# Linear attention with two expert layers: the sums over keys with features stationary, and a new plan

## The chip, the core and the metric

One core of a Trainium2 chip runs the whole program in one launch. TensorE (PE) multiplies matrices, VectorE (DVE), ScalarE (ACT) and GpSimd (POOL) do elementwise work, SyncE (SP) issues most loads and stores. The metric is device time in microseconds, the median of several runs.

## The reference

```python
def phi(x):
    proj = np.einsum('bhsd,df->bhsf', x, w_phi)
    proj = proj - np.max(np.abs(proj), axis=-1, keepdims=True)
    return np.concatenate([np.exp(proj), np.exp(-proj)], axis=-1)
q_p, k_p = (phi(q), phi(k))
kv = np.einsum('bhsf,bhsd->bhfd', k_p, v)
z = np.sum(k_p, axis=2)
num = np.einsum('bhsf,bhfd->bhsd', q_p, kv)
den = np.einsum('bhsf,bhf->bhs', q_p, z)[..., None] + 1e-06
x = num / den
...
h = x @ w_in
x = (h - np.tanh(h)) @ w_out
...
for e in range(E):
    h = np.maximum(x @ w1[e], 0.0)
    out += p[:, e:e + 1] * (h @ w2[e])
```

There are 4 batches, 8 heads, 576 positions and a head dimension of 64; `w_phi` has 128 columns, so a key or query has 256 features (128 of exp(+) and 128 of exp(-)). The attention output, 2304 tokens by 512, goes through a layer of 2048 hidden units and then through four experts of 1024, weighted by normalised probabilities. Everything is float32. `kv` and `z` are what this document calls the sums over keys: per head, 256 features by 64 value columns and one column of plain feature sums.

## The kernel before

The program has two parts. The first, attention and the layer with tanh, is not written in the order in which it runs. The code calls `add` (on the class `Issue`) for every step: its engine, an estimated duration, a function that emits its instructions, the steps it depends on, the ring buffers and PSUM banks it holds, and a mode of TensorE's array ("rows" for matmuls on half of the array's rows, "columns" for half of its columns, "all" otherwise). `Issue.run` then plays the graph through with those estimates and emits the instructions in the order in which the steps start there. Where several steps of one engine are ready, the one with the lowest key goes first; the keys come from the table `DUE`, one number for each step in the order of the `add` calls. A change of array mode is given `SWITCH` us there, and where TensorE is idle in that play between 5 and 45 us, `fill` emits dummy matmuls of the identity, one for each `T_FILL` (0.22 us). The second part, the experts, is written out by hand after `g.run()`.

`k_task(b, p)` handles the keys of two heads (a pair) of one batch: 16 tasks. It loads k and v, transposes k, projects it with `wphi` (a head on each half of the rows), takes the largest absolute value per key, subtracts it and takes both exponentials into `kp` (four keys a partition, 512 keys) and `kpr` (the other 64 keys of both heads). Then come the sums. In `mmk` the values are the stationary operand, 64 columns wide, one head on each half of the array's columns, and the features move, 256 wide: five matmuls a head. For `z`, VectorE first adds the features of four keys into `ks` (three additions a head, through the helper `tt`) and `mmz` multiplies the result with `ones`; in three tasks of the first batch (`SUM_0 = (0,)` leaves out p = 1, 2, 3) `mmz_all` multiplies all features with `ones` instead. The result lies with value columns on the partitions; ScalarE copies it to `kvT`, four transposes (`back`) bring features onto the partitions, and two copies write `kv`, whose last two columns are `z`.

`q_task(b, s, p)` handles the queries of a pair over half of the positions (320 or 256): 32 tasks. `mm(ab, x)` forms numerators and denominators: stationary are up to 64 queries' features on a half of the columns, moving are the 66 columns of `kv`. It is one step for exp(+) (`ea`) and one for exp(-) (`eb`). `moe_slot` and `moe_x2` are the first layer's steps, `split3` its three matmuls for each product (line 454 in the profile, whatever calls it). Line 335 is the helper that issues loads and stores, line 326 the helper for additions on VectorE.

Of the kernel before, what the change touches and what calls it, by code (L numbers as in the profile page):

```python
# [9 lines left out]
F32 = mybir.dt.float32  # L10
# [32 lines left out]
K_SUM = ['DVE', 'DVE', 'DVE']  # L43
K_BIAS = ((), (), (), ())
R_BIAS = (0, 0, 0, 0)
SUM_0 = (0,)
# [63 lines left out]

class Buf:
    def __init__(self, t, last, users):
        self.t, self.last, self.users = t, last, users


class Issue:

    HOP = {"PE": 0.055, "ACT": 0.037, "DVE": 0.033, "POOL": 0.08, "SP": 0.1}  # L120
    DRAIN = {"PE": 0.16, "ACT": 0.11, "DVE": 0.082, "POOL": 0.035, "SP": 0.0}
    SWITCH = 0.125
    T_FILL = 0.22
    fill = None

    def __init__(self, banks, lent):

        self.nodes, self.free_banks, self.lent = [], list(range(banks)), banks
        self.free_lent, self.n_lent = list(range(banks, banks + lent)), lent

    def add(self, eng, dur, fn, deps=(), due=0.0, bufs=(), bank=None, banks=(), frees=(), busy=None, early=0.0, home=False, mode="all", port=False, wire=False):
        x = Node()
        x.home, x.mode, x.port, x.wire = home, mode, port or eng == "POOL", wire or eng == "SP"
        x.eng, x.dur, x.busy, x.fn, x.banks, x.key = eng, dur, busy or dur, fn, [bank] if bank else list(banks), (due, len(self.nodes))
# [131 lines left out]
def attention_moe_moe_kernel(  # L266
# [65 lines left out]
    def dma(pairs, deps=(), due=0.0, bufs=(), early=0.0, slow=1.0, queue="SP"):  # L332
# [5 lines left out]
        return add(queue, size / 300e3, fn, deps, due, bufs, busy=0.7 * len(pairs), early=early, wire=True)  # L338


    ident = const.tile([128, 128], F32, name="ident")
    wphi = const.tile([128, 128], F32, name="wphi")
    b_m = const.tile([128, 1], F32, name="b_m")
    ones = const.tile([128, 3, 64], F32, name="ones")

    warm = const.tile([128, 24], F32, name="pad")[:, 0:1]
    edge.tile([128, 24], F32, name="pad_right")
    vtiles = [att.tile([128, 10 * 64], F32, name=f"vbuf{i}") for i in range(2)]

    make_identity(nc, ident)  # L350
    for _ in range(WARM):
        PE.matmul(accs[0][:, 0:128], lhsT=ident, rhs=ident, start=True, stop=True)
    DVE.memset(b_m, THETA2)
    DVE.memset(ones, 1.0)
    DVE.memset(ones[64:128, 1], 0.0)
    DVE.memset(ones[0:64, 2], 0.0)
    for vb in vtiles:
# [909 lines left out]
```

## Time and profile before

| | |
|---|---|
| median of 3 runs | 1376.47 us (1376.26 to 1376.79) |
| the profiled execution | 1376.24 us |
| its span, first to last instruction | 1374.5 us |
| TensorE busy | 1362.8 us, 99% |
| VectorE, ScalarE, GpSimd busy | 69%, 49%, 47% |
| granted TensorE clock, mean | 0.999 |

The span is what the instructions cover, the rest of the execution's time lies around it. Busy time counts an engine as busy while at least one of its instructions runs. Matmuls are pipelined and overlap in the records, so what a group of them costs is read from its first start to the start of what follows, not from the length of the records. A matmul of float32 operands leaves two records, a transpose one.

### The profile page before, as it was taken

How to read it: one execution, taken by the hardware profiler on the slowest of the kernel's cores; microseconds unless marked ns; L12 is line 12 of the kernel's file. 1: busy time of each engine (PE TensorE's matmuls, PEld its weight loads, DVE VectorE, ACT ScalarE, POOL GpSimd, SP SyncE). 2: the span in 40 equal slices, each digit the busy share in tenths (PEclk: the TensorE clock that was granted, in tenths of full speed). 3: DMA queues.
4: the chain of work that ended last, by engine and by line, in shares of the span. 5: the costliest groups of instructions: out<-in, count | busy, mean ns of one | idle time of the engine just before them, and what ended most of it. 6: DMA issues, size and time to landing. Idle time of an engine off the chain costs nothing.

```text
span 1374.5 us, 23988 instructions
## 1 busy us (share of the span) xinstructions
PE 1362.8 (99%) x9082; PEld 1238.8 (90%) x9082; DVE 948.1 (69%) x1815; ACT 670.2 (49%) x1511; POOL 639.1 (47%) x588
## 2 busy tenths in 40 slices
PE   9999999999999999999999999999999999999998
PEld 7778888889999999998999889998999899998897
DVE  6999988888788676676555556655555575555553
ACT  7877677676575454454333334433333343333331
POOL 1212100112242135234766777777666786677760
PEclk9999999999999999999999999999999999999999
DMA  6634223523378114012212222332222222212211
GB/s 174 193 104 147 69 70 103 192 79 139 134 252 267 56 57 121 29 36 100 77 62 62 77 68 70 108 113 72 77 62 62 77 93 93 62 62 77 69 39 47
DMA packets 130291, 132.34 MB, mean 96 GB/s; under 512 B 51328, under 2 KB 104960, under 8 KB 130176
## 3 DMA queue, kind: packets, MB, share of 16 engines
q1 hardware_dynamic: 129184, 130.44, 29.7%
q8 instruction: 72, 1.18, 0.4%
q10 hardware_dynamic: 992, 0.37, 0.1%
q14 instruction: 43, 0.35, 0.1%
HBM read 104.96 MB, written 25.82 MB: 95 GB/s over the span
## 4 chain that ended last, share of the span: by engine, by line
PE 94%; DVE 4%; ACT 1%; issue 0%; DMA 0%; POOL 0%; DVEq 0%; ACTq 0%; POOLq 0%
PE acc L454 43%; PE bank L454 38%; PE bank L700 2%; PE bank L602 2%; PE bank L668 1%; PE bank L682 1%; PE bank L540 1%; DVE hsm L753 1%; PE bank L718 1%; PE acc L700 1%; PE acc L602 1%; PE bank L657 0%; DVE hsm L751 0%; DVE km L546 0%; DVE kd L558 0%
## 5 line engine op out<-in xcount | busy, mean ns | idle before, releaser
L1187 ACT ACTIVATE h<-xc 128x384 fp32r<-128x384 f32 x160 | 84.1, 526 | 340.6 <-DVE xc L1191 337.7
L1068 POOL TENSOR_TENSOR wslot<-raw,wslot 128x512 fp32r<-128x512 f32 x96 | 138.6, 1459 | 216.7 <-ACT wslot L1067 209.3
L454 PE MATMUL acc<-ghm,wslot 128*128 128x384 f32 (+2 forms) x896 | 234.5, 322 | 3.0 <-ACT ghm L756 2.4
L454 PE MATMUL acc<-wslot,h 128*128 128x512 f32 x960 | 228.0, 389 | 0.0
L454 PE MATMUL bank<-xmem,wslot 128*128 128x384 f32 (+2 forms) x1212 | 217.9, 312 | 1.0 <-DVE kd L558 0.7
L454 PEld LDWEIGHTS acc<-wslot,h 128*128 128x128 f32 x960 | 180.2, 188 | 37.4
L327 POOL TENSOR_TENSOR glm<-thm,ghm 128x384 fp32r<-128x384 f32 (+2 forms) x71 | 67.6, 952 | 289.7 <-ACT ghm L756 230.1
L454 PEld LDWEIGHTS bank<-xmem,wslot 128*128 128x128 f32 x1212 | 184.3, 189 | 3.9 <-DVE kd L558 1.3
L1188 DVE SCALAR_TENSOR_TENSOR h<-xc,h 128x384 fp32r<-128x384 f32 x160 | 112.8, 705 | 94.7 <-ACT h L1187 94.7
L454 PEld LDWEIGHTS acc<-ghm,wslot 128*128 128x128 f32 x896 | 158.8, 188 | 11.7 <-issue 5.3
L1146 DVE SCALAR_TENSOR_TENSOR yacc<-acc,pr,yacc 128x512 f32<-128x512 f32 x83 | 62.1, 750 | 143.0 <-PE acc L454 143.0
L454 PE MATMUL acc<-glm,wslot 128*128 128x384 f32 (+2 forms) x448 | 140.1, 313 | 0.9 <-POOL glm L327 0.6
L1047 POOL TENSOR_TENSOR wslot<-wtmp,wslot 128x512 fp32r<-128x512 f32 x96 | 123.6, 1307 | 0.2 <-ACT wslot L1045 0.2
L1191 DVE TENSOR_TENSOR xc<-bank,xc 128x384 f32<-128x384 f32 x201 | 110.8, 552 | 15.4 <-PE bank L454 9.1
L454 PE MATMUL bank<-wslot,h 128*128 128x512 f32 x480 | 118.2, 392 | 0.0
L1047 POOL TENSOR_TENSOR wslot<-raw,wslot 128x512 fp32r<-128x512 f32 x96 | 99.1, 1051 | 25.5 <-ACT wslot L1045 25.5
L454 PEld LDWEIGHTS bank<-wslot,h 128*128 128x128 f32 x480 | 89.5, 188 | 17.3
L755 DVE COPY_PREDICATED thm<-sqm,hsm 128x384 f32<-128x384 int32 (+2 forms) x112 | 68.9, 618 | 26.9 <-ACT sqm L754 26.4
L454 PEld LDWEIGHTS acc<-glm,wslot 128*128 128x128 f32 x448 | 84.6, 189 | 1.6 <-DVE glm L326 0.8
L756 ACT ACTIVATE ghm<-thm 128x384 fp32r<-128x384 f32 (+2 forms) x112 | 53.1, 478 | 60.9 <-PE acc L454 35.2
L754 ACT ACTIVATE sqm<-sqm,b_m 128x384 f32<-128x384 f32 (+2 forms) x112 | 63.3, 569 | 38.6 <-DVE hsm L753 37.3
L1191 DVE TENSOR_TENSOR xc<-acc,xc 128x384 f32<-128x384 f32 x135 | 74.5, 552 | 10.0 <-PE acc L454 5.9
(271 smaller groups left out, 2987.5 us busy)
## 6 DMA issues: line engine op xcount, KB each, us to landing
raw<-in_moe_w_dram SPq DMA_DIRECT2D x96, 512.0 KB
raw<-in_moe_w_out_dram SPq DMA_DIRECT2D x16, 512.0 KB
raw<-in_moe_w_in_dram SPq DMA_DIRECT2D x16, 512.0 KB
xs<-xmem SPq DMA_DIRECT2D x8, 640.0 KB
out_dram<-yacc SPq DMA_DIRECT2D x17, 256.0 KB
kraw<-in_k_dram SPq DMA_DIRECT2D x16, 256.0 KB
vbuf<-in_v_dram SPq DMA_DIRECT2D x16, 256.0 KB
xs<-xmem SPq DMA_DIRECT2D x8, 512.0 KB
```

What stands on the lines that cost most here:

```text
L327: return add("POOL", c_pool(n), lambda: POOL.tensor_tensor(out=o, in0=a, in1=b, op=op), deps, due, bufs)
L454: PE.matmul(ps, lhsT=a, rhs=b, start=start and n == 1, stop=stop and n == 3 * len(pairs))
L602: PE.matmul(at(bk2)[64 * e:64 * e + 64, 0:256], lhsT=w, rhs=x.rearrange("p a f -> p (a f)"), start=j == 0, stop=j == 4)
L754: x3 = add("ACT", c_act(N, ptr=True), lambda: ACT.activation(out=sq.t, in_=sq.t, func=ACTF.Relu, scale=-1.0, bias=b_m[:, 0:1]), [y3], due ...
L755: y4 = add("DVE", c_dve(N), lambda: DVE.copy_predicated(out=th.t, mask=sq.t.bitcast(I32), data=hs.t), [x3, y2, y3], due + G_AT[6], [th, sq ...
L756: x4 = add("ACT", c_act(N), lambda: ACT.activation(out=gh.t, in_=th.t, func=ACTF.Copy), [y4], due + G_AT[7], [th, gh])
L1047: steps.append(("POOL", c_pool(n), lambda h=h, l=l, src=src: POOL.tensor_tensor(out=l, in0=src, in1=f32(h), op=ALU.subtract)))
L1068: steps += [("POOL", c_pool(DM), lambda c=c: POOL.tensor_tensor(out=vl[:, c], in0=r[:, c], in1=f32(vh[:, c]), op=ALU.subtract)) for c in r ...
L1146: DVE.scalar_tensor_tensor(out=acc[t], in0=y, scalar=pe, in1=acc[t], op0=ALU.mult, op1=ALU.add)
L1187: ACT.activation(out=hh, in_=src, func=ACTF.Relu)
L1188: DVE.scalar_tensor_tensor(out=hl, in0=src, scalar=0.0, in1=f32(hh), op0=ALU.max, op1=ALU.subtract)
L1191: DVE.tensor_tensor(out=o, in0=bk, in1=a, op=ALU.add)
```

## The change

The sums over keys are formed the other way round. The features are stationary, 64 of them on each half of the array's columns, and the values move, 66 columns wide: 64 values, a column of ones, which gives `z`, and one more. Each head's two kinds of features take five key groups and two halves each, 40 matmuls a task. The result lies in PSUM as `kv` is needed, and one copy of 264 columns writes it. The additions into `ks`, `ones`, `kvT` and the transposes back are gone. `vbuf` has a row of 66 used columns (96 apart) for each key group, whose columns 64 and 65 are set to one at the start; v is loaded by four transfers a task instead of three. The two numerator steps of a q task are one step, which waits for both exponentials and `kv`, and not for the scale factors `s2`; VectorE's first product waits for those instead. `SWITCH` is 0.17, a few VectorE steps are marked as sharing a port with GpSimd in the play, and the table `DUE` is new throughout (its first entries were 20.94, -230.95, -162.75 and are 0, 0.7, 4.9), so that all steps of the first part are ordered anew. A line of the second part is not touched.

```diff
-K_SUM = ['DVE', 'DVE', 'DVE']
...
-SUM_0 = (0,)
...
-    SWITCH = 0.125
+    SWITCH = 0.17
...
-    ones = const.tile([128, 3, 64], F32, name="ones")
...
-    vtiles = [att.tile([128, 10 * 64], F32, name=f"vbuf{i}") for i in range(2)]
+    vtiles = [att.tile([128, 2, 5, 96], F32, name=f"vbuf{i}") for i in range(2)]
...
-    DVE.memset(ones, 1.0)
-    DVE.memset(ones[64:128, 1], 0.0)
-    DVE.memset(ones[0:64, 2], 0.0)
     for vb in vtiles:
-        DVE.memset(vb[64:128, 512:576], 0.0)
-        DVE.memset(vb[0:64, 576:640], 0.0)
+        DVE.memset(vb[:, :, :, 64:66], 1.0)
+        DVE.memset(vb[64:128, 0, 4], 0.0)
+        DVE.memset(vb[0:64, 1, 4], 0.0)
...
-    kvT_r = ring(att, 1, [128, 512], F32, "kvT")
...
-    ks_r = ring(att, 2, [128, 256], F32, "ks")
...
-            (vv[:, 0:512].rearrange("p (h x) -> p h x", h=2), v[b, h:h + 2, 0:512, :].rearrange("h (p r) d -> p h (r d)", r=4)),
-            (vv[0:64, 512:576], v[b, h, 512:S, :]),
-            (vv[64:128, 576:640], v[b, h + 1, 512:S, :]),
-        ], due=t0 - 4, bufs=[vb], slow=1.3)
+            (vv[:, e, 0:4, 0:64], v[b, h + e, 0:512, :].rearrange("(p r) d -> p r d", r=4)) for e in range(2)
+        ] + [
+            (vv[64 * e:64 * e + 64, e, 4, 0:64], v[b, h + e, 512:S, :]) for e in range(2)
+        ], due=t0 - 4, bufs=[vb], slow=2.2)
...
-        kss, zs = [], []
-        summed = b > 0 or p in SUM_0
-        for e in range(2 if summed else 0):
-            kp, kd, ks = kps[e], kds[e], ks_r.take()
-            tz = kd.t.rearrange("p j f -> p (j f)")
-            h0 = 64 * e
-
-            a = tt(K_SUM[0], tz, kp.t[:, 0:2].rearrange("p j a f -> p (j a f)"), kp.t[:, 2:4].rearrange("p j a f -> p (j a f)"), ALU.add, 512, es[e], t0 + K_PACE * (K_AT[12] + e) + nudge(12), [kp, kd])
-            a = tt(K_SUM[1], ks.t, tz[:, 0:256], tz[:, 256:512], ALU.add, 256, [a], t0 + K_PACE * (K_AT[13] + e) + nudge(13), [kd, ks])
-            zs.append(tt(K_SUM[2], ks.t[h0:h0 + 64], ks.t[h0:h0 + 64], kpr.t[h0:h0 + 64].rearrange("p a f -> p (a f)"), ALU.add, 256, [a, r1, r2], t0 + K_PACE * (K_AT[14] + e) + nudge(14), [ks, kpr]))
-            kss.append(ks)
-        bk2, bk3, kvT, kv = Bank(), Bank(), kvT_r.take(), kv_r.take()
+        bk2, kv = Bank(), kv_r.take()
 
         def mmk():
-            for j in range(5):
-                for e in range(2):
-                    w = vv[:, 512 + 64 * e:576 + 64 * e] if j == 4 else vv[:, 256 * e + 64 * j:256 * e + 64 * j + 64]
-                    x = kpr.t if j == 4 else kps[e].t[:, j]
-                    PE.matmul(at(bk2)[64 * e:64 * e + 64, 0:256], lhsT=w, rhs=x.rearrange("p a f -> p (a f)"), start=j == 0, stop=j == 4)
-
-        def mmz():
             for e in range(2):
-                PE.matmul(at(bk2)[64 * e:64 * e + 64, 256:512], lhsT=ones[:, 0], rhs=kss[e].t, start=True, stop=True)
-
-        def mmz_all():
-            for j in range(5):
-                for e in range(2):
-                    x = kpr.t if j == 4 else kps[e].t[:, j]
-                    PE.matmul(at(bk2)[64 * e:64 * e + 64, 256:512], lhsT=ones[:, 1 + e if j == 4 else 0], rhs=x.rearrange("p a f -> p (a f)"), start=j == 0, stop=j == 4)
-
-        def back():
-            for i in range(4):
-                PE.transpose(out=at(bk3)[:, i * 128:(i + 1) * 128], in_=kvT.t[:, i * 128:(i + 1) * 128], identity=ident)
-
-        def kv_out(lo, n):
-            return kv.t[:, :, :, lo:lo + n].rearrange("p e a d -> p a e d")
-
-        def kv_in(i, n):
-            return at(bk3)[:, 256 * i:256 * i + 256].rearrange("p (a e d) -> p a e d", a=2, e=2)[:, :, :, 0:n]
-
-        def mm_all():
-            mmk()
-            (mmz if summed else mmz_all)()
-
-        a = add("PE", 2.6 if summed else 4.3, mm_all, [*es[0], *es[1], r1, r2, ldv, *zs], t0 + K_PACE * K_AT[15] + nudge(15) if summed else t0 + K_PACE * K_AT[16] + nudge(16), [*kps, *kss, kpr, vb, kvT], bank=bk2, mode="columns")
-        a = add("ACT", c_act(512, True), lambda: ACT.activation(out=kvT.t, in_=at(bk2), func=ACTF.Copy), [a], t0 + K_PACE * K_AT[17] + nudge(17), [kvT], frees=[bk2])
-        a = add("PE", 0.44, back, [a], t0 + K_PACE * K_AT[18] + nudge(18), [kvT, kv], bank=bk3)
-        a1 = add("ACT", c_act(256, True), lambda: ACT.activation(out=kv_out(0, 64), in_=kv_in(0, 64), func=ACTF.Copy), [a], t0 + K_PACE * K_AT[19] + nudge(19), [kv], frees=[bk3])
-        a2 = add("ACT", 0.1, lambda: ACT.activation(out=kv_out(64, 2), in_=kv_in(1, 2), func=ACTF.Copy), [a], t0 + K_PACE * K_AT[20] + nudge(20), [kv], frees=[bk3])
-        kv_of[b, p] = (kv, [a1, a2])
+                for x in range(2):
+                    o = (2 * e + x) * DV
+                    for j in range(5):
+                        kf = kpr.t[:, x] if j == 4 else kps[e].t[:, j, x]
+                        for c in (0, 64):
+                            PE.matmul(at(bk2)[c:c + 64, o:o + DV], lhsT=kf[:, c:c + 64], rhs=vv[:, e, j, 0:DV], start=j == 0, stop=j == 4)
+
+        a = add("PE", 40 * (2 * DV + 8) / 2400.0, mmk, [*es[0], *es[1], r1, r2, ldv], t0 + K_PACE * K_AT[15] + nudge(15), [*kps, kpr, vb, kv], bank=bk2, mode="columns")
+        a = add("ACT", c_act(4 * DV, True), lambda: ACT.activation(out=kv.t.rearrange("p e a d -> p (e a d)"), in_=at(bk2)[:, 0:4 * DV], func=ACTF.Copy), [a], t0 + K_PACE * K_AT[17] + nudge(17), [kv], frees=[bk2])
+        kv_of[b, p] = (kv, [a])
...
-        pm = [add("PE", R * 4 * (2 * DV + 8) / 2400.0, lambda ab=ab, x=x: mm(ab, x), [xe[ab], *([] if ab else [s2]), *kvdone], t0 + Q_PACE * Q_AT[9] + nudge(9) + 0.5 * ab, [x, kv, ub], bank=nb[ab], mode="columns") for ab, x in enumerate((ea, eb))]
+        def both():
+            mm(0, ea)
+            mm(1, eb)
+
+        pm = add("PE", R * 8 * (2 * DV + 8) / 2400.0, both, [*xe, *kvdone], t0 + Q_PACE * Q_AT[9] + nudge(9), [ea, eb, kv, ub], banks=nb, mode="columns")
 
         due = t0 + Q_PACE * Q_AT[10] + nudge(10)
         nd = 2 * R * DV
-        a = add("DVE", c_dve(nd), lambda: DVE.tensor_tensor(out=u, in0=side(0), in1=qse[:, 0].unsqueeze(3).to_broadcast([QP, 2, R, DV]), op=ALU.mult), [pm[0], s2], due, [qs, ub], frees=[nb[0]])
-        a = add("DVE", c_dve(nd), lambda: DVE.tensor_tensor(out=u, in0=side(1), in1=u, op=ALU.add), [a, pm[1]], due, [ub], frees=[nb[1]])
+        a = add("DVE", c_dve(nd), lambda: DVE.tensor_tensor(out=u, in0=side(0), in1=qse[:, 0].unsqueeze(3).to_broadcast([QP, 2, R, DV]), op=ALU.mult), [pm, s2], due, [qs, ub], frees=[nb[0]])
+        a = add("DVE", c_dve(nd), lambda: DVE.tensor_tensor(out=u, in0=side(1), in1=u, op=ALU.add), [a], due, [ub], frees=[nb[1]])
...
-            last = [add("DVE", c_dve(2 * NL), lambda i=i: x_diff(i), last, due + 2 + i)]
+            last = [add("DVE", c_dve(2 * NL), lambda i=i: x_diff(i), last, due + 2 + i, port=True)]
...
-            last = [add(eng, dur, fn, [*last, *(free if i == wait else [])], t2 - 14 + 4 * n if n < 2 else t2 + n, tiles)]
+            last = [add(eng, dur, fn, [*last, *(free if i == wait else [])], t2 - 14 + 4 * n if n < 2 else t2 + n, tiles, port=eng == "DVE")]
```

What the new plan does to the order is seen at three places.

TensorE, a task of sums in the middle of the first part (`kp`, `kpr` features, `xf` the attention output, `pq` projected queries, `ea` and `eb` their exponentials, `wslot` the layer's weights). Before:

```order
L602 MATMUL bank_85<-kp_191,vbuf_95 64x256
L602 MATMUL bank_85<-kpr_193,vbuf_95 64x256 x2
L606 MATMUL bank_85<-ks_201,ones 64x256
L606 MATMUL bank_85<-ks_202,ones 64x256
L718 MATMUL bank_84<-ident,xf_219 128x107 x3
L700 MATMUL bank_87<-kv_199,eb_209 64x66 x8
L616 MATMUL bank_85<-ident,kvT_194 128x128 x4
L524 MATMUL bank_86<-ident,krawr_179 64x128
L682 MATMUL bank_84<-ident,pq_205 128x128 x2
```

The end of the value matmuls and the two with ones are followed by a transpose, by numerators, and only then by the transposes back of the same task. With the change:

```order
L559 MATMUL bank_85<-wphi,kTr_181 128x128
L585 MATMUL bank_87<-vbuf_93,kp_188 64x66 x8
L585 MATMUL bank_87<-vbuf_93,kpr_190 64x66 x2
...
L585 MATMUL bank_87<-vbuf_93,kp_189 64x66 x8
L585 MATMUL bank_87<-vbuf_93,kpr_190 64x66 x2
...
L656 MATMUL bank_85<-kv_193,ea_203 64x66
L656 MATMUL bank_85<-kv_193,ea_203 43x66
...
L656 MATMUL bank_86<-kv_193,eb_205 64x66
...
L516 MATMUL bank_84<-ident,krawr_176 64x128
L513 MATMUL bank_87<-ident,kraw_174 128x128 x4
```

Forty narrow matmuls stand together, 24 numerator matmuls of another task stand right behind them, and no transposes back follow.

TensorE within the first steps, where dummy matmuls (`ident` with `ident`) fill the play's idle time. Before:

```order
L657 MATMUL bank_84<-ident,qraw_181 128x112 x3
L1087 MATMUL bank_85<-ident 128x128 x4
L682 MATMUL acc_83<-ident,pq_205 107x128 x3
L524 MATMUL acc_81<-ident,krawr_179 64x128
L521 MATMUL acc_80<-ident,kraw_177 128x128 x4
L682 MATMUL acc_82<-ident,pq_205 107x128 x3
L567 MATMUL acc_83<-wphi,kTr_183 128x128
L1087 MATMUL bank_85<-ident 128x128 x9
L668 MATMUL acc_81<-qx_204,wphi 128x320
L668 MATMUL acc_82<-qx_204,wphi 128x320
```

There are 21 dummy matmuls in all before. With the change, somewhat later in the program, ahead of the second task's sums:

```order
L613 MATMUL bank_84<-ident,qraw_179 128x112 x3
L1047 MATMUL bank_85<-ident 128x128
L624 MATMUL acc_83<-qx_198,wphi 128x320
L624 MATMUL acc_82<-qx_198,wphi 128x320
L559 MATMUL acc_81<-wphi,kTr_181 128x128
L1047 MATMUL bank_85<-ident 128x128 x5
L638 MATMUL acc_80<-ident,pq_200 107x128 x3
L1047 MATMUL bank_85<-ident 128x128 x2
L638 MATMUL acc_82<-ident,pq_200 107x128 x3
L1047 MATMUL bank_85<-ident 128x128 x10
L516 MATMUL acc_83<-ident,krawr_177 64x128
L585 MATMUL acc_82<-vbuf_94,kp_188 64x66 x8
```

There are 33 in all; 18 of them stand in this piece.

SyncE at the start of the program: k, v and q of the first tasks. Before:

```order
L335 DMA kraw_176<-in_k_dram 128x8x64
L335 DMA krawr_178<-in_k_dram 128x1x64
L335 DMA vbuf_94<-in_v_dram 128x2x256
L335 DMA vbuf_94<-in_v_dram 64x64 x2
L335 DMA qraw_181<-in_q_dram 112x6x64
L335 DMA kraw_177<-in_k_dram 128x8x64
L335 DMA krawr_179<-in_k_dram 128x1x64
```

The second k follows one load of v and one of q. With the change:

```order
L333 DMA qraw_179<-in_q_dram 112x6x64
L333 DMA kraw_174<-in_k_dram 128x8x64
L333 DMA krawr_176<-in_k_dram 128x1x64
L333 DMA vbuf_94<-in_v_dram 128x4x64 x2
L333 DMA vbuf_94<-in_v_dram 64x64 x2
L333 DMA vbuf_93<-in_v_dram 128x4x64 x2
L333 DMA vbuf_93<-in_v_dram 64x64 x2
L333 DMA kraw_175<-in_k_dram 128x8x64
L333 DMA krawr_177<-in_k_dram 128x1x64
L333 DMA kraw_174<-in_k_dram 128x8x64
```

q comes first, and both tasks' loads of v, four transfers each, stand ahead of the second k.

## Rows read from the trace of the kernel before

**Rows 1.** The chain that ended last, by engine, over the whole span (the page).

```profile
PE 94%; DVE 4%; ACT 1%; issue 0%; DMA 0%; POOL 0%; DVEq 0%; ACTq 0%; POOLq 0%
```

**Rows 2.** Stretches of the span: us, busy us of each engine, clock, DMA share, GB/s.

```profile
0.00:15.00 15.00, 13.66 (x104) 12.00 (x104) 8.31 (x26) 8.34 (x19) 0.69 (x6) 1.00 0.72 171
...
60.00:120.00 60.00, 58.34 (x638) 48.88 (x634) 58.48 (x143) 46.13 (x121) 5.89 (x5) 1.00 0.43 136
...
630.00:1374.50 744.50, 740.80 (x3723) 670.84 (x3721) 433.97 (x690) 266.53 (x526) 492.35 (x459) 1.00 0.23 74
```

**Rows 3.** What TensorE (PE) waited for, first and last of eleven rows.

```profile
PE acc L454 <- ACT ghm L756: 2.4, 3, 1.3
...
PE acc L454 <- DVE glm L326: 0.2, 1, 0.2
```

**Rows 4.** TensorE's timeline, 222 to 229 us: start, us, operation, records.

```profile
222.27 1.95 PE L602 MATMUL bank<-kp,vbuf 128*64 128x256 f32 x16
224.05 0.60 PE L602 MATMUL bank<-kpr,vbuf 128*64 128x256 f32 x4
224.48 0.60 PE L606 MATMUL bank<-ks,ones 128*64 128x256 f32 x4
224.91 0.64 PE L700 MATMUL bank<-kv,eb 128*64 128x66 f32 x16
...
225.95 0.66 PE L616 MATMUL bank<-ident,kvT 128*128 128x128 f32 x4
226.36 0.36 PE L454 MATMUL acc<-ghm,wslot 128*128 128x256 f32 x1
...
227.34 0.91 PE L700 MATMUL bank<-kv,ea 128*64 128x66 f32 x24
228.07 0.88 PE L700 MATMUL bank<-kv,eb 128*43 128x66 f32 x24
228.88 1.16 PE L540 MATMUL bank<-wphi,kT 64*128 64x128 f32 x16
```

**Rows 5.** TensorE's timeline, 25 to 31 us.

```profile
25.38 1.95 PE L602 MATMUL acc<-kp,vbuf 128*64 128x256 f32 x16
...
27.59 1.90 PE L612 MATMUL acc<-kp,ones 128*64 128x256 f32 x16
...
29.85 0.49 PE L718 MATMUL acc<-ident,xf 107*128 107x107 f32 x3
```

**Rows 6.** TensorE's timeline around 200 and 213 us.

```profile
200.29 1.68 PE L454 MATMUL bank<-xmem,wslot 128*128 128x256 f32 x12
201.89 0.81 PE L668 MATMUL bank<-qx,wphi 64*128 64x320 f32 x4
...
212.93 4.47 PE L454 MATMUL bank<-xmem,wslot 128*128 128x256 f32 x36
217.25 0.44 PE L718 MATMUL bank<-ident,xf 107*128 107x107 f32 x3
```

**Rows 7.** TensorE's timeline, 9 to 11 us.

```profile
9.78 1.07 PE L1087 MATMUL bank<-ident 128*128 128x128 f32 x8
10.69 0.49 PE L682 MATMUL acc<-ident,pq 128*107 128x128 f32 x3
```

**Rows 8.** Groups by line and tile: busy us, mean ns, idle before.

```profile
L673 ACT ACTIVATE ea<-pq 128x640 f32<-128x640 f32 (+1 forms) x32 | 22.0, 688 | 0.2
...
L326 DVE TENSOR_TENSOR kd<-kp 128x512 f32<-128x512 f32 x26 | 18.3, 707 | 2.4 <-ACT kp L559 2.3
...
L326 DVE TENSOR_TENSOR ks<-ks,kpr 64x256 f32<-64x256 f32 x26 | 11.4, 439 | 0.4
...
L326 DVE TENSOR_TENSOR ks<-kd 128x256 f32<-128x256 f32 x26 | 10.7, 415 | 0.1
```

**Rows 9.** DMA queue: packets, MB, share of 16 engines (the page).

```profile
q1 hardware_dynamic: 129184, 130.44, 29.7%
```

**Rows 10.** Groups by line and tile, the numerators' matmuls.

```profile
L700 PE MATMUL bank<-kv,eb 128*64 128x66 f32 (+1 forms) x528 | 20.9, 225 | 0.6 <-DVE u L708 0.6
```

2 lines of the change are left out of this document (1 added, 1 removed).

## The prediction

> **What bounds the kernel now.** I read the chain of waits first: 94% of the span is TensorE's own work [rows 1]. The table by stretches says the same of each stage [rows 2]: TensorE is busy 13.66 of the first 15 us, 58.34 of 60 us between 60 and 120 us, 740.80 of the last 744.5 us. Its list of waits has eleven rows, the longest 2.4 us, the last 0.2 us, 7.9 us together [rows 3]. So a microsecond of TensorE work that goes away shortens the run, unless a wait takes its place; work on other engines counts only through such waits. The nearest to a second bound is VectorE, busy 58.48 of 60 us from 60 to 120 us [rows 2]. The last 744.5 us are the hand-written second layer, in which no line is touched: the change acts in the first 630 us alone, mostly before 430 us, where attention is woven into the first layer.
>
> Busy time of pipelined matmuls overlaps, so I price TensorE by the time from one group's start to the next one's start in its timeline. Each fp32 matmul leaves two records there, each transpose one.
>
> **Sums over keys, before.** In a task whose features were added on VectorE first, the ten value matmuls (20 records) run from 222.27 to 224.48: 2.21 us; the two with ones (4 records) to 224.91: 0.43 us; the four transposes back from 225.95 to 226.36: 0.41 us [rows 4]. That is 3.05 us, and 13 of the 16 tasks are so: 39.7 us. In the other three the ones are multiplied with all features: from 25.38 to 29.85 is 4.47 us for both halves [rows 5], of which some 0.1 is a change of array mode (priced below); 4.37 + 0.41 = 4.78 us, three times 14.3 us. Together 54.0 us.
>
> **Sums over keys, after.** Forty matmuls of 66 moving columns, on halves of the array's columns. The trace has that shape: the q task's numerator, where 64 or 43 stationary columns meet the same 66 columns of kv. There 24 records take 227.34 to 228.07, 0.73 us, or 30.4 ns a record [rows 4]. Eighty records are 2.43 us, 16 tasks 38.9 us. **Saved: 15.1 us.** The work moved is about equal (per task 20 pairs of 66 columns against 5 of 256); what is saved is the separate pass with ones and the way back. Two matmuls in step cost 0.43 us at 256 columns (four records of the ones) and 0.122 us at 66: 1.62 ns a column and 15 ns fixed, so cutting into narrower pieces costs little. I take the row as it stands, since it has the same stationary and moving widths; what differs is that five matmuls now accumulate in the same columns. The value matmuls do that already at 0.108 us a record [rows 4].
>
> **Changes of array mode.** TensorE's steps use half the rows (feature projections), half the columns (sums over keys, numerators) or the whole array. In the issue order I count 184 changes from one such mode to another before and 118 after: the new plan puts sums and numerators next to each other, both numerators are one step now, and the transposes back no longer interrupt. What one costs: 24 numerator records take 0.73 us when column work follows and 0.81 us, from 228.07 to 228.88, when row work follows [rows 4], 0.08 us; twelve matmuls of 256 columns take 1.60 us ahead of row work (200.29 to 201.89), while 36 of them take 4.32 us, that is 1.44 for twelve, ahead of whole-array work [rows 6], 0.16 us. I take the middle, 0.12 us: 66 times 0.12 = **7.9 us saved**, with 5.3 and 10.6 as ends.
>
> **Fillers.** The planner puts dummy matmuls where it sees TensorE idle between 5 and 45 us. The order holds 21 before and 33 now. Four of them (8 records) take from 9.78 to 10.69, 0.228 us each [rows 7]: twelve more are **2.7 us added**. They say that the first 45 us hold less ready work, as the sums shrink there and two loads of v now stand ahead of the second k.
>
> **Beside the path, costed at nothing.** VectorE loses three additions for each of 26 heads, 18.3 + 10.7 + 11.4 = 40.4 us [rows 8], all under TensorE today; they stood between the exponentials and the sums, so a task is ready earlier by two of these chains at most. If VectorE was what made TensorE wait, some of the 7.9 us of waits goes too; that is the low end. ScalarE has one copy of 264 columns in place of three. SyncE issues one load more per task, and the main part of v lands in pieces of 256 instead of 1024 bytes: 768 more packets a task. The queue's mean packet is 50.6 ns (29.7% of 16 engines' span over 129,184 packets [rows 9]), so at most 768 x 50.6 / 16 = 2.4 us of all DMA engines per task, hidden while their share is 0.72 in the first 15 us and 0.43 between 60 and 120 us [rows 2]; without that cover it is a wait ahead of the sums. The joint numerator step now waits for both exponentials, where its first half waited for one: at most one exponential, 0.688 us [rows 8], 32 times 22 us, if it always came last; behind it stand the next steps of TensorE, and VectorE's product waits for it. At least nothing: it no longer waits for the scale factors, which only VectorE's product does now. I take nothing, since the planner orders it when both are due.
>
> **Sum.** -15.1 - 7.9 + 2.7 = -20.3 us. The profiled execution took 1376.24 us (span 1374.5 and 1.7 around it), 0.23 under the median of the runs shown: 1376.24 - 20.3 = **1355.9 us**, 1.5% faster. A measurement of this kernel can tell about 0.2%, 2.8 us, from no change.
>
> **Rivals.**
> *The new order waits more.* Every step of the first 630 us has a new place, and 16 sums and 32 numerators each stand ahead of everything later on TensorE. Against it: VectorE is relieved by 40.4 us and banks are held less, and the old order shows that such a plan can run with 7.9 us of waits [rows 3]. For it: no row of this trace shows the new order, and its first 15 us are the thinnest part (13.66 of 15 us busy [rows 2], fillers included). At 0.6 us a sum the waits are 9.6 us and the time 1365.5; at 1.27 us a sum the whole gain is gone.
>
> *The narrow matmuls do not keep the pace of the numerators* (this one ends slower). Place: the 40 pairs of records per task that accumulate five deep in 66 columns. If each had to end before the next pair begins, it would take the whole 225 ns of a record [rows 10]: 40 x 0.225 = 9.0 us a task, 144 us in all, 105 us more than I counted, 1461 us. It decides from 32 ns more per pair of records (20.3 us over 640), 93 ns in place of 61. Against it: both records of one numerator matmul already go to the same columns at that pace, and the value matmuls accumulate five deep without a gap [rows 4].
> A rule of the Trainium skill points the same way: the page TensorEngine Tiling (Array Packing), section Instruction Overhead, gives each matmul about 60 cycles of overhead. As an estimate from that page, 25 ns (60 cycles at 2.4 GHz) on each of 1280 records is 32 us, and the sum would end at 1388 us. The numerators' 30.4 ns for a record, overhead included, leave no room for it, so by the trace it does not hold for this shape.
>
> *It gives more.* Mode changes at the upper end (10.6 us) and waits that go with VectorE's 40.4 us: 1376.24 - 15.1 - 10.6 + 2.7 is 1353.2, and less all 7.9 us of waits 1345.3 us.
>
> That the change does not do what it says is excluded by the order: 640 of the narrow matmuls, none of the old sums.
>
> **How the numbers follow.** My case, with mode changes between 5.3 and 10.6 us and up to 4 us of new waits, spans 1353 to 1362 us: 71%. The order that waits (1362 to 1374, typically 1365): 18%, of which a tail reaches no change. More gain, under 1353: 7%. Slower by the narrow matmuls: 4%. The range 1350 to 1365 leaves out about half of the second case, some of the third and all of the fourth, together under 2 in 10. Faster by over 0.2%: 95%; within it 2%, the tail of the waiting order; slower 3%, most of the last case.
>
> **What would show it.** Right: the 40 matmuls of one task from first start to next step in 2.4 to 2.5 us; no transposes of kvT and no additions into ks; groups of sums directly followed by numerators; TensorE's waits within a few us of 7.9; the stretch up to the second layer shorter by 20 us, and the 744.5 us behind it the same. Wrong: sums of 3 us or more (the narrow matmuls), waits ahead of the sums or loads of v in the list of waits (the order), or a mode change that costs nothing, in which case the time is 1363 or 1364 us.

## The result, and the profile after

| | before | after |
|---|---|---|
| median, same chip | 1376.63 us (1376.26 to 1377.16) | **1345.99 us** (1345.56 to 1347.7) |
| ratio, 95% interval | | 0.9779 (0.9763 to 0.9796) |
| the profiled execution; its span | 1376.24 us; 1374.5 us | 1345.56 us; 1343.8 us |
| changes of array mode; fillers | 184; 21 | 118; 33 |

The kernel is 30.6 us faster. The forecast was 20.3 us; the time lies 4 us under the foot of the range, where the third rival ("it gives more") stood.

The changed kernel's chain that ended last, and its list of what TensorE waited for, all eight rows (us in total, times, longest):

```profile
PE 96%; DVE 2%; ACT 1%; issue 0%; POOL 0%; DVEq 0%; ACTq 0%; POOLq 0%
```

```profile
PE acc L348 <- POOL ident masks.py:199: 1.3, 1, 1.3
PE acc L678 <- DVE kd L550: 1.0, 1, 1.0
PE acc L656 <- ACT kv L588: 0.6, 1, 0.6
PE acc L624 <- ACT qx L626: 0.5, 1, 0.5
PE bank L448 <- ACT pq L628: 0.2, 1, 0.2
PE bank L638 <- DVE qm L641: 0.2, 1, 0.2
PE bank L656 <- DVE qm L641: 0.2, 1, 0.2
PE acc L638 <- ACT pq L628: 0.2, 1, 0.2
```

That is 4.2 us where before had 7.9 [rows 3]. The three waits for `ghm`, 2.4 us together, are gone; two of them, 2.2 us, stood behind attention, in a stretch that now has no row at all. `kv L588` is the new copy of 264 columns: numerators waited for it once, 0.6 us.

One task's sums in the changed kernel's timeline of TensorE (start, us, operation, records):

```profile
102.49 0.69 PE L585 MATMUL bank<-vbuf,kp 128*64 128x66 f32 x16
103.01 0.29 PE L585 MATMUL bank<-vbuf,kpr 128*64 128x66 f32 x4
...
104.97 1.16 PE L532 MATMUL bank<-wphi,kT 64*128 64x128 f32 x16
```

From 102.49 to 104.97: 80 records in 2.48 us, forecast 2.43. Where numerators follow, in the same array mode, it is 2.38 us (85.09 to 87.47), 29.8 ns a record; the numerators before had 30.4 [rows 4]. The Trainium skill, TensorEngine Tiling (Array Packing), section Instruction Overhead, gives each matmul about 60 cycles of overhead. As an addition of 25 ns to every record, which is how the prediction's estimate from that page reads it, it does not show here: the sums cost what the rows gave without it. That a record every 29.8 ns leaves no room for it does not follow, though: the two halves of the columns work at once, and each half starts a record only every 59.5 ns. What speaks against it is the prediction's own sum from two widths, 15 ns fixed for four records.

The span in three stretches: attention woven into the first layer (up to the first 384-wide matmul on `xmem`), the rest of the first layer, the second layer (from its first matmul on `xo`). Columns as in [rows 2]. Before:

```profile
0.00:417.80 417.80, 412.85 (x4157) 360.76 (x4158) 361.75 (x866) 294.71 (x764) 77.77 (x74) 1.00 0.44 141
417.80:626.10 208.30, 205.22 (x1184) 203.25 (x1183) 150.64 (x258) 107.91 (x219) 65.13 (x54) 1.00 0.27 84
626.10:1374.50 748.40, 744.70 (x3746) 674.74 (x3744) 435.68 (x693) 267.55 (x528) 496.25 (x462) 1.00 0.23 75
```

After:

```profile
0.00:392.70 392.70, 388.31 (x4967) 363.07 (x4968) 323.25 (x783) 278.85 (x726) 71.01 (x70) 1.00 0.48 144
392.70:595.70 203.00, 203.00 (x1181) 203.00 (x1180) 152.45 (x262) 111.79 (x226) 66.89 (x55) 1.00 0.31 98
595.70:1343.80 748.10, 744.44 (x3746) 674.73 (x3744) 435.36 (x693) 267.44 (x528) 498.74 (x464) 1.00 0.24 75
```

25.1 us come from the first stretch, 5.3 from the second, 0.3 from the third. The second holds none of the sums: TensorE had 3.1 us of idle there and now has none. In the kernel before, most of that idle time lay in the last 8 us of the stretch (from the timelines of VectorE, ScalarE and TensorE; in brackets the engine's idle time ahead of a step and what ended it):

```profile
612.54 1.52 DVE L1043 TENSOR_TENSOR wtmp<-raw 128x256 f32<-128x256 f32 x1
...
615.00 1.51 DVE L1043 TENSOR_TENSOR wtmp<-wtmp,raw 128x256 f32<-128x256 f32 x1
616.43 1.53 DVE L1043 TENSOR_TENSOR wtmp<-raw 128x256 f32<-128x256 f32 x1
617.88 0.41 DVE L1043 TENSOR_TENSOR wtmp<-raw,wtmp 128x256 f32<-128x256 f32 x1
618.22 0.57 DVE L755 COPY_PREDICATED thm<-sqm,hsm 128x384 f32<-128x384 int32 x1
```

```profile
618.82 0.52 ACT L756 ACTIVATE ghm<-thm 128x384 fp32r<-128x384 f32 x1 [1.76 <-DVE thm L755]
```

```profile
619.40 0.44 PE L454 MATMUL acc<-ghm,wslot 128*128 128x384 f32 x1 [0.88 <-ACT ghm L756]
```

VectorE prepares weights for the experts (`wtmp`) ahead of the `thm` that `ghm`, and then TensorE, waits for. With the new keys two of these four steps stand behind the last `thm` of the stretch:

```profile
590.40 1.68 DVE L715 COPY_PREDICATED thm<-sqm,hsm 128x384 f32<-128x384 int32 x1
591.97 0.41 DVE L1003 TENSOR_TENSOR wtmp<-raw 128x256 f32<-128x256 f32 x1
592.30 0.42 DVE L1003 TENSOR_TENSOR wtmp<-raw,wtmp 128x256 f32<-128x256 f32 x1
```

Three of the four steps before took 1.5 us each, while GpSimd ran its own subtractions for the same weights (612.12 to 617.67 us), and the last, behind those, 0.41 us. That the place of the four made the wait is read from the timelines; it was not tested by itself.

To compare kernels I go through the starts of TensorE's records in each trace. A record's usual distance to the next one of its kind is its work; what is over at a change of mode is the price of the change; what is over by a gap of more than 60 ns is waits; the remainder is small hold-ups ("rest"). Sums and fillers are thus counts times a usual distance. In us:

| | sums | fillers | mode changes | waits | rest | first stretch | second |
|---|---|---|---|---|---|---|---|
| before | 53.6 | 4.8 | 25.4 (184) | 10.3 | 7.2 | 417.8 | 208.3 |
| after | 38.1 | 7.5 | 15.6 (118) | 4.3 | 5.2 | 392.7 | 203.0 |
| change's sums, old keys | 38.1 | 13.0 | 22.9 (159) | 36.0 | 8.1 | 434.8 | 207.8 |
| old sums, new keys | 53.6 | 6.8 | 22.3 (162) | 23.3 | 9.4 | 434.5 | 205.7 |
| numerators split | 38.1 | 7.3 | 20.5 (143) | 11.0 | 9.1 | 406.4 | 203.9 |
| before, new late keys | 53.6 | 4.8 | 25.5 (184) | 7.9 | 8.8 | 420.2 | 204.2 |
| before, no additions | 53.6 | 4.8 | 25.2 (184) | 8.6 | 8.1 | 416.7 | 208.4 |
| after, additions' load back | 38.1 | 7.5 | 22.4 (118) | 32.4 | 7.5 | 430.0 | 203.0 |

What the five columns leave of the profiled span is 1273.1 to 1273.2 us in every one. Before to after: sums -15.5, fillers +2.7, mode changes -9.8, waits -6.0, rest -2.0. The last three columns are not cleanly apart: the kernel in the last row has the same order on TensorE as the change, with the same 118 mode changes, and yet 22.4 us stand there in place of 15.6, since short waits that end at a change count with it. Waits are more here than in the profile's own list (10.3 against 7.9 us before), which counts idle time between modelled ends.

### The profile page after: what moved, and what is told of

Read it like the earlier page. It is cut to its first block, busy times and chain, and to the rows that moved or that the text cites. A ratio compares the mean times of both kernels' runs of the same rounds, so it can differ in the third digit from the quotient of the medians.

```text
span 1343.8 us, 25514 instructions
## 1 busy us (share of the span) xinstructions
PE 1335.8 (99%) x9890; PEld 1240.8 (92%) x9890; DVE 911.1 (68%) x1736; ACT 658.1 (49%) x1479; POOL 636.6 (47%) x588
## 4 chain that ended last, share of the span: by engine, by line
PE 96%; DVE 2%; ACT 1%; issue 0%; POOL 0%; DVEq 0%; ACTq 0%; POOLq 0%
PE acc L448 45%; PE bank L448 40%; PE bank L656 2%; PE bank L585 2%; PE bank L638 1%; PE bank L624 1%; PE bank L532 1%; PE bank L678 1%; PE bank L1047 1%; PE bank L613 0%; PE acc L585 0%; PE bank L513 0%; DVE km L538 0%; DVE kd L550 0%; PE acc L532 0%
## 5 line engine op out<-in xcount | busy, mean ns | idle before, releaser
L715 DVE COPY_PREDICATED thm<-sqm,hsm 128x384 f32<-128x384 int32 (+2 forms) x112 | 73.4, 658 | 29.5 <-ACT sqm L714 29.1
L1151 DVE TENSOR_TENSOR xc<-acc,xc 128x384 f32<-128x384 f32 x135 | 74.5, 552 | 10.3 <-PE acc L448 5.9
L1003 POOL TENSOR_TENSOR wtmp<-raw 128x256 f32<-128x256 f32 x90 | 80.5, 894 | 0.0
```

What stands on the lines that cost most here:

```text
L715: y4 = add("DVE", c_dve(N), lambda: DVE.copy_predicated(out=th.t, mask=sq.t.bitcast(I32), data=hs.t), [x3, y2, y3], due + G_AT[6], [th, sq ...
L1003: steps = [(adder, 0.36, lambda o=o, a=a, b=b, op=op: {"DVE": DVE, "POOL": POOL}[adder].tensor_tensor(out=o, in0=a, in1=b, op=op)) for o, ...
L1151: DVE.tensor_tensor(out=o, in0=bk, in1=a, op=ALU.add)
```

## The experiments

Ratios are to the kernel before, measured on the same chip together with each run, where its median was 1376.6 to 1377.7 us.

**Parts with each other's keys.** First the change's sums and joint numerators with the old table of keys:

```diff
-DUE = [0, 0.7, 4.9, ...]
+DUE = [20.94, -230.95, -162.75, ...]
-    SWITCH = 0.17
+    SWITCH = 0.125
```

> The change's sums and its joint numerator step, with the keys of the plan before (each step keeps the key of the step it replaces). The order then holds 159 changes of array mode (184 before, 118 with the change) and 57 dummy matmuls (21 and 33). Theory A, each part adds: sums -15.9 us (16 tasks of 2.38 us in place of 54.0 us), 25 changes of mode fewer at 0.135 us are -3.4, 36 more dummies at 0.228 us are +8.2, the waits of the old keys stay: 1376.6 - 11.1 = 1365.5 us (1361 to 1369). Theory B, the sums are the whole gain and the new keys bring nothing: 1346 to 1350 us.

Measured 1394.01 us, ratio 1.0116 (1.0100 to 1.0133). The reverse keeps the old sums and the two numerator steps, and takes the new keys (steps that the change lacks get the key of their neighbour):

> The sums of the kernel before (additions on VectorE, ones, transposes back, two numerator steps) with the keys of the new plan. 162 changes of mode, 30 dummies. Theory A: against before, 22 changes of mode fewer are -3.0 us, nine dummies more +2.1, the waits that the new keys avoid -6: about 1369.7 us (1366 to 1373). Theory B, the new keys bring nothing without the new sums: 1376 us or more.

Measured 1391.44 us, ratio 1.0097 (1.0082 to 1.0112). The first kernel missed both theories; the second missed A by 22 us and lies on B's side, 15 us beyond its bound. The sums kept their price (in the first kernel a task's 80 records take 2.33 to 2.48 us to the next step); the waits did not: 36.0 and 23.3 us. Of these, 6.6 and 5.6 us are what records that started while the granted clock was at its lower level, 1.2 GHz, took over their usual distance; the mean clock was 0.995 and 0.996. The first rows of the waits of the change's sums with old keys:

```profile
PE acc L450 <- ACT ghm L721: 10.0, 6, 2.7
PE acc L450 <- POOL glm L327: 1.9, 3, 0.8
PE acc L450 <- DVE glm L326: 1.5, 4, 0.7
```

It is mostly the first layer's own products that are late (line 450, 15.6 of the 23.0 us in the list), not the sums (2.1 us). So these steps and these keys fit only each other, and neither half is worth anything alone. A table made anew for the old sums, or for the new ones without the joint step, was not tried; how much of the gain better keys could have given to the old steps is open.

**The joint numerator alone.** The change with its numerators as two steps again, both with the joint step's key:

```diff
-        pm = add("PE", ..., both, [*xe, *kvdone], ..., mode="columns")
+        pm0 = add("PE", ..., lambda: mm(0, ea), [xe[0], s2, *kvdone], ..., mode="columns")
+        pm = add("PE", ..., lambda: mm(1, eb), [xe[1], *kvdone], ..., mode="columns")
```

> The changed kernel with the two numerator steps apart again (the first waits for its own exponential and the scale factors, as before). 143 changes of mode in place of 118, one dummy fewer. Theory A, a change of mode costs about 0.135 us: +3.4 - 0.2, 1349.2 us. At the 0.08 us of the lowest row it is 1347.8, at 0.17 us 1350.0. Theory D, the joint step costs waits that the split one does not have: under 1346 us.

Measured 1360.52 us, ratio 0.9866 (0.9851 to 0.9881), 14.5 us over the change and more than either theory gave. 25 more mode changes cost 4.9 us in the table, 0.196 each, which is over theory A's upper price and so has some waiting in it; the rest is waits (+6.7) and small hold-ups (+3.9). Again the mode changes are near what was counted, and the waits of a new order are not.

**The late keys alone.** The kernel before, in which only the last 978 keys come from the new table:

```diff
-DUE = DUE_old
+DUE = DUE_old[:-978] + [x + 100 for x in DUE_new[-978:]]
```

> The kernel before with the new plan's keys for the last 978 steps alone (behind attention: the rest of the first layer and the loading for the second); TensorE's order up to the last attention step is that of before, and so are the mode changes. Theory A, the late waits (3 us seen as idle before 533 to 624 us, 5.3 us by the length of that stretch) belong to the late keys: 1371 to 1374 us. Theory C, they go only because attention ends earlier or its queues are emptier: 1376.6 us, no change. The price of the late part is then seen by subtraction.

Measured 1374.81 us, ratio 0.9980 (0.9971 to 0.9990): a part of what A expected. Its first two stretches:

```profile
0.00:420.20 420.20, 414.03 (x4156) 362.07 (x4157) 363.07 (x866) 294.93 (x764) 77.93 (x74) 1.00 0.44 140
420.20:624.40 204.20, 203.81 (x1185) 203.50 (x1184) 153.67 (x258) 108.31 (x219) 63.88 (x52) 1.00 0.28 85
```

The second stretch falls from 208.30 to 204.20 us, 4.1 of the change's 5.3, with not one sum changed; the first stretch and the last give 3.3 us back (417.8 to 420.2, 748.4 to 749.3). With the old late keys the second stretch is 207.8 to 209.7 us in every kernel, whichever sums it has; with the new ones 203.0 to 205.7 in all but one (the rank of 150 us, below, whose added steps reach into it). So the second stretch's 5.3 us come with the keys. As a net gain the late keys alone are worth less, 0.8 us between the profiled spans and 2.8 between the medians.

**What a change of mode costs.** One unused product of the identity (whole array) between the two heads of each task's sums, and as a control the same product ahead of the transposes of k, where the mode does not change:

```diff
             for e in range(2):
+                if e == 1:
+                    PE.matmul(at(bk2)[:, 384:512], lhsT=ident, rhs=ident, start=True, stop=True)
```

> The change as it is, with one unused 128-column product of the identity, a whole-array matmul, put between the two heads of each task's sums: 16 such products and 32 more changes of array mode, in work that waits for nothing in between. One product costs 0.23 us by the fillers, 16 are 3.6 us. Theory A (a mode change costs 0.13 to 0.14 us wherever it stands): 32 are 4.3 us, together 1346.0 + 3.6 + 4.3 = 1353.9 us; at the prediction's 0.12 us 1353.4 us. Rival (a mode change costs nothing by itself, and the 66 that went took with them only the restarts of steps that waited): 1349.6 us.

> The control for the products between the heads: the same 16 unused products, each ahead of the four whole-array transposes of a task's k, so that no mode change is added. Both theories: at most 3.6 us over the changed kernel, 1349.6 us; less where TensorE would have waited there anyway. By theory A the kernel with the products between the heads is 4.3 us above this one, by the rival 0 us.

Measured 1355.39 us, ratio 0.9843 (0.9830 to 0.9857), and 1350.50 us, ratio 0.9812 (0.9798 to 0.9825). The same task in both timelines, the control first:

```profile
68.81 0.69 PE L586 MATMUL acc<-vbuf,kp 128*64 128x66 f32 x16
...
71.29 0.44 PE L679 MATMUL acc<-ident,xf 128*128 128x128 f32 x2
```

With the product between the heads:

```profile
71.02 0.69 PE L587 MATMUL acc<-vbuf,kp 128*64 128x66 f32 x16
...
72.12 0.29 PE L587 MATMUL acc<-vbuf,kpr 128*64 128x66 f32 x4
72.33 0.49 PE L581 MATMUL acc<-ident 128*128 128x128 f32 x2
72.75 0.69 PE L587 MATMUL acc<-vbuf,kp 128*64 128x66 f32 x16
...
74.07 0.44 PE L680 MATMUL acc<-ident,xf 128*128 128x128 f32 x2
```

2.48 us become 3.05. Less the product's own 0.228 us [rows 7] that is 0.34 us for two changes, **0.17 us each**; the spans say the same, (1353.5 - 1348.0) / 32 = 0.17, and the medians 0.15. The control itself came out 0.9 us over its bound. The starts of the single records show where the 0.34 us lie: 100 ns ahead of the product, 101 behind its first record, 93 ahead of the second head, and 50 in that head's first pair of records. So a change costs time twice, before the new mode's first record and right behind it. In this task TensorE waits for nothing in either, so the rival of a free mode change falls. The Trainium skill, TensorEngine Tiling (Array Packing), section Key Properties, says that changing the mode drains TensorE and gives no price; the trace agrees, with this one.

**Fillers.** The changed kernel without its 33 dummy matmuls (`FILL = (5.0, 5.0)`):

> The changed kernel without its 33 dummy matmuls between 5 and 45 us, 7.5 us of TensorE work. Theory A (they stand where TensorE would wait anyway): 1345.5 to 1346.5 us, with as many us of waits more in the first 45 us. Rival (they hold up work that was ready): as far as 1338.5 us, if all of them do; 1343.3 us, if only the twelve new ones do.

Measured 1346.92 us, ratio 0.9786 (0.9772 to 0.9799), 0.9 us over the change: 7.5 us of fillers went, waits rose from 4.3 to 12.8 (in the profile's own list from 4.2 to 8.5). Theory A holds in the main, 0.4 us over its bound. So the +2.7 us of fillers in my sum were mostly idle time by another name. Not all of the 8.5 us need be waiting: the granted clock of the first 45 us, 1.00 in the change, was 0.96 without the fillers.

**VectorE's 40.4 us.** The prediction costed them at nothing. First from the side of the old kernel, its order untouched:

```diff
-            return add("DVE", c_dve(n), lambda: DVE.tensor_tensor(out=o, in0=a, in1=b, op=op), ...)
+            return add("DVE", c_dve(n), lambda: None, ...)
```

> The kernel before, every instruction in its old place, but VectorE's three additions of each of the 26 heads are left out (the ones are multiplied with a constant tile instead, so the denominators are not computed). TensorE, ScalarE, POOL and SP keep their order; VectorE has 78 instructions and 40.4 us less. Theory A (the additions lay beside the path, the prediction's step): 1375.5 to 1377 us, TensorE's waits still about 8 us. Theory B (VectorE's additions were what made TensorE wait): the waits before 430 us go and the small stalls with them, 1368 to 1372 us.

Measured 1375.47 us, ratio 0.9988 (0.9979 to 0.9996). Theory A: the additions cost the old kernel 1 to 2 us, and the second stretch stays at 208.4 us, so they were not what made TensorE wait there. Then from the side of the changed kernel:

```diff
                 DVE.tensor_tensor(out=kd.t, ..., op=ALU.subtract)
+                if b > 0 or p == 0:
+                    for w in (512, 256, 256):
+                        DVE.tensor_tensor(out=scr[:, 0:w], in0=scr[:, 0:w], in1=scr[:, 0:w], op=ALU.add)
```

> The change as it is, with VectorE's old additions put back as load alone: behind the subtraction of each of the 26 heads that had them, additions of 512, 256 and 256 columns in a scratch tile that nobody reads. TensorE's order stays the changed kernel's. VectorE does 40 us more, some 950 us of busy time again. Theory A (the 6 us of waits went because VectorE was relieved): they come back, 1350 to 1353 us, with VectorE's work named ahead of TensorE's waits. Theory B (waits follow from how keys and steps fit, and VectorE's additions lay beside the path): 1345 to 1348 us.

> The changed kernel with the additions put back as load behind each of the 26 subtractions, but of 256, 64 and 64 columns: some 0.7 us a head in place of 1.55, 18 us in all. The full load of 40.4 us cost 36 us. Theory A (VectorE has no slack in the attention part, every microsecond put ahead of its row counts): half as much, 1362 to 1366 us. Theory B (the plan has slack of several us, and only what goes over it counts): 1346 to 1353 us.

Measured 1382.26 us, ratio 1.0041 (1.0028 to 1.0053), and for the half 1363.01 us, ratio 0.9898 (0.9882 to 0.9913). Both theories of the first missed, the load cost 36 us; the half of it cost 17, as its theory A said. TensorE's work did not change; the first three of the full load's rows of waits:

```profile
PE acc L664 <- DVE kTr L523: 3.6, 1, 3.6
PE bank L686 <- DVE u L676: 2.4, 2, 1.6
PE bank L515 <- DVE qm L649: 1.7, 1, 1.7
```

Is that VectorE's total, or the place? The old kernel with its additions moved to that same place, the total unchanged:

> The kernel before with its three additions per head taken from their old places and put, as load alone, behind the subtraction of the same head (the ones are multiplied with a constant tile, so the denominators are not computed). VectorE's total is that of the kernel before; the place is the one that cost the changed kernel 36 us. Theory A (the place costs: what stands ahead of a head's exponentials and of the next maximum holds up TensorE whatever VectorE's total): 1385 to 1400 us. Theory B (VectorE's total is what counts, and the old plan has room for this total): 1375 to 1380 us.

Measured 1407.90 us, ratio 1.0222 (1.0208 to 1.0236): 31 us from the place alone. So I gave the changed kernel the load as steps that nobody waits for, with three ranks:

```diff
+                for w in (512, 256, 256):
+                    y = add("DVE", c_dve(w), lambda w=w: DVE.tensor_tensor(out=scr[:, 0:w], ...), [x1, y], ...)
+                    g.late[y] = x2, LATE    # key: that of x2 plus LATE, 4, 20 or 150 us
```

> The changed kernel with the full additions as load again (40.4 us), but as steps of their own that the planner knows: ready when a head's exponentials are done, keyed 4 us behind the second one, with nobody who waits for them. The order has 131 mode changes in place of 118 (13 x 0.15 = 2 us). Theory A (VectorE's time itself is short): 1360 to 1383 us. Theory B (it is the place ahead of the next maxima and exponentials that cost 36 us; where VectorE can choose, its additions lie beside the path): 1346 to 1352 us.

> The same, keyed 20 us behind the second exponential; 136 mode changes (18 x 0.15 = 2.7 us). Theory A: 1360 us or more. Theory B: between the rank of 4 us (1373.9 us) and that of 150 us, 1350 to 1365 us.

> As the kernel whose additions are steps of their own, keyed 4 us behind the second exponential, but keyed 150 us behind it: VectorE takes them only when nothing of the next 150 us is ready. 131 mode changes (13 x 0.15 = 2 us over the changed kernel). Theory A (the changed plan has no room for 40.4 us of VectorE's time at any place): still 1360 us or more. Theory B (it has the room, and only the rank of the additions cost 28 to 36 us): 1346 to 1353 us.

Measured: rank 4 us 1373.85 us, ratio 0.9969 (0.9959 to 0.9979); rank 20 us 1373.30 us, ratio 0.9965 (0.9953 to 0.9978); rank 150 us 1360.88 us, ratio 0.9875 (0.9860 to 0.9890). The last one's first two stretches:

```profile
0.00:400.20 400.20, 393.50 (x4949) 362.81 (x4950) 352.45 (x861) 277.69 (x723) 70.60 (x68) 1.00 0.46 140
400.20:611.40 211.20, 207.82 (x1200) 207.32 (x1199) 154.99 (x263) 113.12 (x229) 69.03 (x57) 0.99 0.31 96
```

By its number theory A (1360 or more) holds, barely; by the stretches neither is clean. The attention stretch carries 29 us more of VectorE than the change and is only 7.5 us longer; 8.2 us more are lost behind it, where new waits stand, the longest this one:

```profile
PE acc L449 <- DVE x2m L850: 3.0, 1, 3.0
```

So rank is worth 13 us (the load costs 28 us at 4 and 15 at 150; some 2 of either are the 13 mode changes more). Whether keys made for this load would bring the 15 us down was not tried and stays open.

No kernel of this study is faster than the change.

## Why the prediction was right and wrong

**Right, by its steps.** The sums: -15.1 forecast, -15.5 measured; the row of the numerators' matmuls carried over to five deep accumulation. The fillers: +2.7 and +2.7. The way back and the additions are gone, and v's smaller pieces cost nothing: no wait for v stands in the list. ScalarE's copy was taken at nothing and shows once, 0.6 us. The second layer: 748.4 and 748.1 us.

**Right in number, not in its reason: the count of mode changes.** 184 and 118 are so. But sums and numerators do not stand together more than before: of 16 tasks, numerators directly follow the sums in 4 before and in 3 after, and directly precede them in 3 and 5. The place shown ahead of the prediction is one of the three. The other reasons carry the count: split again, the numerators alone bring back 25 of the 66, and 16 groups of transposes back are gone.

**A term mis-sized: the price of a mode change.** The prediction took 0.12 us, the middle of 0.08 and 0.16 [rows 4, 6]. The 66 that went gave 9.8 us in the table, 0.148 each, and 0.15 to 0.17 was measured by itself, which would be 10 to 11 us. By the table it is 1.9 us of the 10.3 that the sum missed. The upper end was near the truth, but by luck, as the starts of the records show. In the row of 0.08 us the group of 0.73 us itself begins behind a change (its first pair takes 97 ns, the later ones some 58), which took 0.04 us off, and what the row work behind the other group loses in its own first pair (213 ns in place of 112) was not counted. In the row of 0.16 us some 0.08 is no change of mode: the first of the twelve matmuls starts 28 ns behind a transpose, where 110 is usual, and is held that much longer, 202 ns in place of 120.

**The step that failed: the waits.** "The change acts in the first 630 us alone, mostly before 430 us", and its existing waits, 7.9 us, were taken to stay. By the table 6.0 us of waits and 2.0 of small hold-ups went, 8.0 of the 10.3 (1 to 2 us less where a mode change is taken at 0.17); the last 0.4 are the sums. Most of the 8.0 lies where no step was changed: the second stretch, 5.3 us, from 208.3 to 203.0, through the new keys (shown by the late keys alone, 4.1 us). The prediction had the row in hand, `ghm` for 2.4 us at the top of the list [rows 3], but asked only whether the removed work caused it, not what the new order would do to it. Its one route to fewer waits, VectorE's relief, is not the cause in that stretch: without the additions it stays at 208.4 us. What took the remaining 2.7 us, in the first stretch, was not told apart.

**VectorE, costed at nothing.** For the old order that was right, 1 to 2 us. As a statement on the change it was too simple: the changed plan, 25 us shorter in the first stretch, uses the time that the additions left (with them VectorE would be busy 323.25 + 40.4 of 392.7 us, by this estimate 93%, against 87% before). With them back it keeps between none and 55% of its gain in the four places tried. The gain on TensorE and the relief of VectorE are not two terms that add.

**The rivals.** "The new order waits more" was false of this order, though the two kernels with keys that don't belong to their steps show how near it lay: 36 and 23 us of waits. The narrow matmuls kept their pace. "It gives more" came true with its first half (the mode changes' upper end), and with its second half in size; for the larger part of that, the second stretch, not in cause.

## What to carry to other kernels

Price the work on the bounding engine from rows of the same shape, and it comes out to a few tenths of a microsecond; price waits from the new order as a whole, stretch by stretch, since a new table of keys also moves what the change does not touch. Parts of such a change can't be judged one at a time: both halves alone were slower than the kernel before. Work on a second engine may be free to remove and dear to put back, so test its cost in the plan that you mean to run.

## What was not expected of the hardware

A change between array modes costs 0.13 (the mean over the changed kernel's 118) to 0.17 us (measured by itself, where nothing waits), as much as four to six of the 66-column records.

When TensorE was held up, its clock fell as well. In the changed kernel with the additions' load back (columns as above, the seventh number behind the stretch is the granted clock):

```profile
40.00:50.00 10.00, 9.02 (x197) 7.94 (x195) 9.96 (x22) 9.99 (x24) 4.36 (x3) 1.00 0.76 196
50.00:60.00 10.00, 6.42 (x120) 5.99 (x117) 8.86 (x22) 4.70 (x12) 1.49 (x1) 0.70 0.50 131
60.00:70.00 10.00, 10.00 (x130) 8.53 (x130) 8.57 (x27) 6.87 (x22) 0.00 (x0) 0.96 0.45 154
```

TensorE was busy 6.42 of 10 us, and the granted clock was 0.70 of 2.4 GHz on average, part of the stretch at 1.2 GHz. By its table of stretches of 60 us the clock was 0.95, 0.99, 0.94 and 0.97 in four of the first six, so up to 60 x (0.05 + 0.01 + 0.06 + 0.03) = 9 us of its 37 may be clock, the rest is waiting. How much of the 9 fell on idle time the view does not tell; the 163 records that started at the lower clock took 7.6 us more than their usual distance, waits among them, which is a closer bound.
